# A written order of 3,359 operations, replaced by another; shared buffers handed out in that order

## The chip, the core and the metric

The kernel runs on one core of a Trainium2 chip. A core has a matrix engine (TensorE, PE in the views, its weight loads PEld), VectorE (DVE), ScalarE (ACT), GpSimd (POOL) and SyncE (SP, which here only issues DMAs). Each engine takes its own instructions one after the other; between engines, semaphores hold an instruction back until what it needs is there. The metric is the device time of one execution in microseconds, lower is better.

## The reference

```python
# q, k, v: (4, 8, 768, 64); centroids: (8, 16, 64)
q_assign = argmax(einsum('bhsd,hcd->bhsc', q_n, c_n)); k_assign = the same for k
mask   = q_assign[..., :, None] == k_assign[..., None, :]
scores = where(mask, q @ k.T / 8, -1e9)
attn   = softmax(scores) @ v
x      = attn.transpose(0, 2, 1, 3).reshape(3072, 512)
h      = x @ w_in                       # 512 -> 2048
g      = h * tanh(softplus(h))          # mish
out    = g @ w_out                      # 2048 -> 512
```

So there are two parts: attention in which a query sees the keys of its own cluster alone, and a two-layer network over the 3,072 tokens.

## The kernel before, in words

The attention is cut into 96 units (32 heads, three blocks of 256 queries each); each unit is worked in two halves `a` of 128 queries. A half goes from engine to engine: `scores` (PE, four matmuls into a PSUM tile `s`), `rowmax` (DVE), `expo` (ACT, writes `p`), `total` and `recip` (small), and then:

- in the first 24 units: `p_lo` transposes `p` on PE into PSUM tiles `q`, `ptrans` copies them out on ACT or DVE, `pv` multiplies with the raw values (three parts of PE work for two units);
- in the other 72: `p_hi` (POOL) and `p_lo` (DVE) split `p` into two 16-bit numbers `hl`, `ptrans` transposes those by a DMA from SP's queue (`pt<-hl`), `pv` multiplies them with the split values.

`pv_out` and `x_lo` write the result as `x`. The network follows on the same engines, interleaved with the attention: `m1(j, fi)` is a block of 12 matmuls of the first layer (two blocks `fi` fill one PSUM tile `h`), `e_mish(j)` the activation on ACT, `e_gh` (POOL) and `e_gl` (DVE) split it, `m2(k, a, f)` is a block of six matmuls of the second layer, `m_out` and `m_store` bring a result out. The last part of the network goes by Strassen-like products (`c_*`, `l_*`, `n_*`, `k_*`) with `n_mul` and `k_mul` as their matmul blocks. During the first 24 units the weights are loaded and split (`w_load`, `w_abs`, `w_low`, `w_f32`, `w_sq`, `w_hi`, `w_lo`), and for every four heads the clusters are worked out (`assign_*`). For the first head, `hot_direct` brings the cluster pattern into the operands.

Tiles come from pools with a fixed number of buffers. The PSUM tiles matter here: `s` has two, `h` shares two with `q`, and the tile of the second layer and that of `pv` have one each. A new tile waits until a buffer is given back, that is until the last reader of its former tile has run.

The order is written out by hand. Every operation is entered by `pl.at(t, fn, ...)` with a place `t`, worked out from the tables `T`, `N` and, for single operations, `SHIFT`. `Plan.run` sorts by `t` and traces the operations one after the other; an operation that needs another first (`pl.after`) pulls it forward. `tie` then fixes, for each engine, the order in which its instructions were traced. Nothing else decides what an engine does next. Two facts of the code matter for ScalarE:

```python
        if j % 2 == 0 and j <= 72:
            nc.scalar.preload_act_table_set("mish")
        nc.scalar.activation(st["u", j], st["h", j], AF.Mish, scale=vst[j // 24, "h"])
        if j % 2 and j < 72:
            nc.scalar.preload_act_table_set("natural_log_exp_and_others")
```

so the table for `Mish` is loaded before an even `e_mish` and that for `Exp` after an odd one. In the order before, no `expo` stands between the two; where one does, each of the two functions finds the other's table and a load is put in front of it.

Of the kernel before, what the change touches and what calls it, by code (L numbers as in the profile page):

```python
# [25 lines left out]

class Plan:
# [45 lines left out]
def tile_clustered_attention_mish_ffn(  # L73
# [9 lines left out]
    nc = tc.nc  # L83
    pool = lambda name, bufs, **kw: ctx.enter_context(tc.tile_pool(name=name, bufs=bufs, **kw))
# [22 lines left out]
    pl = Plan(tc)  # L107
# [998 lines left out]
    def k_mul(t, n, f):  # L1106
# [3 lines left out]
        if f == 0:  # L1110
# [3 lines left out]
            else:  # L1114
                banks(("k", t))
                ring("k_12", t)
# [130 lines left out]
    for n in range(32):  # L1247
        p = n // 16
        t = N["w"][n]
# [311 lines left out]
SHIFT = {  # L1561
    ('expo', 11, 0): -0.001, ('w_load', 10): -0.351, ('pv_out', 18): -0.443, ('scores', 24, 1): -0.221,
    ('copy_b', 8): 0.081, ('scores', 25, 1): -1.54, ('w_lo', 2): 0.002, ('p_lo', 26, 1): 3.011,
    ('scores', 6, 0): 0.46301, ('recip', 29, 0): 0.006, ('assign_mm', 0): 5.035, ('qk_load', 0): -4.812,
    ('qk_load', 1): 0.018, ('qk_load', 2): -7.858, ('qk_load', 3): 0.077, ('w_f32', 29): 3.258, ('w_low', 18): 0.746,
    ('w_low', 22): -0.606, ('pv', 5, 0): 0.121, ('w_low', 19): -0.124, ('pv_out', 10): 6.683,
    ('v_split', 1, 1): 0.554, ('recip', 8, 1): 0.081, ('recip', 1, 1): 5.617, ('w_hi', 10): -0.185,
    ('rowmax', 18, 1): 0.004, ('total', 7, 1): 0.2, ('w_low', 29): 0.475, ('w_low', 31): 0.855,
    ('total', 14, 1): 0.656, ('w_load', 0): 0.797, ('p_hi', 7, 0): -1.238, ('p_hi', 6, 1): -0.098,
    ('p_hi', 6, 0): 0.511, ('w_low', 21): 3.895, ('pv', 11, 0): 1.133, ('w_f32', 17): -0.084, ('p_hi', 0, 0): 0.06,  # L1570
    ('p_hi', 0, 1): -0.176, ('p_hi', 1, 0): -1.304, ('p_hi', 1, 1): -0.022, ('p_hi', 2, 0): 0.43,
    ('p_hi', 2, 1): -0.009, ('p_hi', 3, 1): -0.009, ('p_hi', 4, 1): -0.002, ('p_hi', 5, 1): -0.01,
# [738 lines left out]
```

## Time and profile before

| | |
|---|---|
| time before, median of 3 runs | 858.68 us (856.95 to 859.97) |
| profiled execution, first to last instruction | 858.6 us |
| PE / DVE / ACT / POOL busy | 837.1 / 702.6 / 520.9 / 428.0 us |
| granted TensorE clock | 1.00 of full speed (the 2.4 GHz level) |
| first score block begins | 15.61 us |
| last matmul, last VectorE operation, last DMA issue | 852.28 (24 matmuls to 855.06), 855.11, 855.62 us |

The profiled execution is the span itself; nothing is shown around it. A busy PE is not a full one: matmuls overlap, and the span of a matmul of 256 columns (0.27 us) is shown while the next one starts 0.11 us later. So an idle gap in the views is a little shorter than the work that was lost in it.

### The profile page before, as it was taken

The numbers are of one execution on the slowest core, as the hardware profiler recorded it, in microseconds if no ns is written. First come the engines' busy times: TensorE is split into PE (matmuls) and PEld (weight loads), VectorE is DVE, ScalarE is ACT, GpSimd is POOL, SyncE is SP. The second block draws the span as 40 slices with busy tenths as digits, with TensorE's granted clock in tenths as the row PEclk, the third lists the DMA queues.
The fourth block names the chain that finished last, engine by engine and source line by source line (L and its number), as shares of the span: only waits on it lengthen the run. The fifth ranks groups of instructions, "written<-read, shape, count | busy, mean of one in ns | idle before, by whom it ended". The sixth has DMA issues, their size and how long they took to land.

```text
span 858.6 us, 17602 instructions
## 1 busy us (share of the span) xinstructions
PE 837.1 (97%) x6742; PEld 621.0 (72%) x6743; DVE 702.6 (82%) x1225; ACT 520.9 (61%) x885; POOL 428.0 (50%) x410
## 2 busy tenths in 40 slices
PE   8999899999999999999999999999999999999998
PEld 3776676776777777776776776776777776788887
DVE  7989989898889798788877798788978777699851
ACT  6878887765665666564565665465565564356520
POOL 1464665786567546556566447566566444110000
PEclk9999999999999999999999999999999999999999
DMA  9855672398889987897789977988887876000010
GB/s 348 262 173 165 193 209 54 73 180 170 149 153 194 193 154 133 156 184 141 145 177 181 172 157 120 171 155 165 130 159 136 139 137 128 24 1 2 1 44 32
DMA packets 253060, 121.51 MB, mean 142 GB/s; under 512 B 230288, under 2 KB 230800, under 8 KB 252976
## 3 DMA queue, kind: packets, MB, share of 16 engines
q1 hardware_dynamic: 247632, 108.46, 61.1%
q10 hardware_dynamic: 5344, 11.93, 6.3%
q8 instruction: 53, 0.87, 0.4%
q14 instruction: 31, 0.25, 0.1%
HBM read 35.72 MB, written 6.29 MB: 49 GB/s over the span
## 4 chain that ended last, share of the span: by engine, by line
PE 70%; DVE 13%; issue 5%; ACT 4%; DMA 4%; POOL 3%; ACTq 0%; POOLq 0%; DVEq 0%; SPq 0%
PE h L832 8%; PE h L833 8%; PE h L834 8%; PE o L753 8%; PE O L969 6%; PE O L971 6%; PE O L970 6%; PE s L631 5%; PE s L636 5%; DVE m L648 4%; PE cn L922 2%; DVE hl L717 2%; DMA pt<-hl 2%; ACT p L662 2%; PE as L543 1%
## 5 line engine op out<-in xcount | busy, mean ns | idle before, releaser
L662 ACT ACTIVATE p<-s,m 128x768 f32<-128x768 f32 x192 | 172.6, 899 | 161.4 <-DVE m L648 108.0
L700 POOL TENSOR_SCALAR hl<-p,l 128x768 f16<-128x768 f32 x144 | 167.1, 1163 | 168.0 <-DVE l L682 74.2
L648 DVE TENSOR_REDUCE m<-s 128x1 f32<-128x768 f32 x192 | 181.4, 949 | 30.2 <-PE s L636 28.1
L717 DVE SCALAR_TENSOR_TENSOR hl<-p,l,hl 128x768 f16<-128x768 f32 x144 | 172.4, 1202 | 12.2 <-POOL hl L700 11.7
L832 PE MATMUL h<-x,w 128*128 128x256 f16 x640 | 175.6, 274 | 1.5 <-ACT u L843 0.8
L833 PE MATMUL h<-x,w 128*128 128x256 f16 x640 | 174.4, 273 | 0.0
L834 PE MATMUL h<-x,w 128*128 128x256 f16 x640 | 174.4, 273 | 0.0
L631 PE MATMUL s<-A,B 128*128 128x384 f32 x384 | 117.3, 386 | 1.8 <-DMA B<-T 0.8
L969 PE MATMUL O<-w,g 128*128 128x512 f16 x288 | 109.6, 380 | 0.0
L971 PE MATMUL O<-w,g 128*128 128x512 f16 x288 | 109.2, 379 | 0.0
L970 PE MATMUL O<-w,g 128*128 128x512 f16 x288 | 109.2, 379 | 0.0
L636 PE MATMUL s<-Z,T 80*128 80x384 f32 x384 | 99.2, 339 | 0.4 <-issue 0.4
L832 PEld LDWEIGHTS <-w 128*128 128x128 f16 x768 | 75.1, 98 | 26.9 <-issue 17.3
L849 POOL TENSOR_SCALAR g<-u,mscg 128x512 f16<-128x512 f32 x72 | 70.3, 980 | 38.4 <-ACT u L843 36.0
L857 DVE SCALAR_TENSOR_TENSOR g<-u,mscg,g 128x512 f16<-128x512 f32 x72 | 75.5, 1050 | 12.2 <-POOL g L849 11.9
L833 PEld LDWEIGHTS <-w 128*128 128x128 f16 x768 | 75.5, 98 | 11.1 <-issue 1.6
L753 PE MATMUL o<-pt,v 128*64 128x256 f16 x1296 | 79.3, 274 | 3.6 <-DMA pt<-hl 3.0
L834 PEld LDWEIGHTS <-w 128*128 128x128 f16 x768 | 75.2, 98 | 8.6
L753 PEld LDWEIGHTS <-v 128*64 128x64 f16 x1296 | 68.4, 110 | 14.1 <-issue 9.6
L631 PEld LDWEIGHTS s<-A,B 128*128 128x128 f32 x384 | 61.9, 190 | 15.8 <-issue 4.9
L636 PEld LDWEIGHTS s<-Z,T 80*128 80x128 f32 x384 | 69.7, 189 | 0.9 <-DMA Z<-stg 0.7
L843 ACT ACTIVATE u<-h,msch 128x512 f32<-128x512 f32 x80 | 52.1, 685 | 25.0 <-PE h L834 14.5
(242 smaller groups left out, 1366.3 us busy)
## 6 DMA issues: line engine op xcount, KB each, us to landing
qk<-in_qk_dram SPq DMA_DIRECT2D x32, 384.0 KB, 4.6
stage<-in_w_in_dram SPq DMA_DIRECT2D x16, 512.0 KB, 6.6
stage<-in_w_out_dram SPq DMA_DIRECT2D x16, 512.0 KB, 4.5
vraw<-in_vP_dram SPq DMA_DIRECT2D x16, 384.0 KB, 5.2
T<-A ACTq DMA_DIRECT2D x30, 192.0 KB, 3.0
Z<-B SPq DMA_DIRECT2D x30, 192.0 KB, 3.4
B<-T ACTq DMA_DIRECT2D x28, 192.0 KB, 3.4
out_dram<-osb SPq DMA_DIRECT2D x18, 256.0 KB, 2.7
```

Source lines behind the costliest of these rows:

```text
L631: nc.tensor.matmul(s[:, j, :384], st["B", n][:, q0 : q0 + P], st["A", n][:, j * 384 : (j + 1) * 384], start=True, stop=False,)
L636: nc.tensor.matmul(s[:, j, :384], st["T", n][: D + NCL, q0 : q0 + P], st["Z", n][: D + NCL, j * 384 : (j + 1) * 384], start=False, stop=True,)
L648: nc.vector.tensor_reduce(m, st["s", i, a][:, :, :384], axis=AX.XY, op=ALU.max, negate=True)
L662: nc.scalar.activation(p.rearrange("p (n x) -> p n x", n=2), st["s", i, a][:, :, :384], AF.Exp, bias=st["m", i, a], scale=1.0, accum_out=l,)
L700: nc.gpsimd.tensor_scalar(t[:, 0], p, r, 1.0, op0=ALU.mult, op1=ALU.mult)
L717: nc.vector.scalar_tensor_tensor(t[:, 1], p, r, t[:, 0], op0=ALU.mult, op1=ALU.subtract)
L753: nc.tensor.matmul(o[s * D : s * D + D, :256], v if early else v[:, int(part == 1)], st["pt", 2 * m + s][:, :, c + (0 if early or part < 2 ...
L832: nc.tensor.matmul(o, wh, xh, start=(c == 0), stop=False)
L833: nc.tensor.matmul(o, wh, xl, start=False, stop=False)
L834: nc.tensor.matmul(o, wl, xh, start=False, stop=(c == 3))
L969: nc.tensor.matmul(o, gh, wh, start=(f == 0 and fi == 0), stop=False)
L970: nc.tensor.matmul(o, gh, wl, start=False, stop=False)
```

## The change

No instruction is added to the program by hand, and none is taken out or reshaped: all 3,359 operations stand with the same work in another order. `pl.at` no longer uses its `t`: it looks the place up in `RANK`, built from one long string `ORDER`. `SHIFT` goes. As every operation stands behind those that it needs, `pl.after` pulls nothing forward any more.

A new class `Ring` wraps each pool and notes when a tile of a tag is asked for; `tie` makes the first instruction of each such tile follow the first one of the tag's tile before, so that buffers are handed out in the order of `ORDER`. The function `ring`, which held back three of the last stage's operations until a buffer's former user had been traced, goes with its three calls.

```diff
+class Ring:
+    def __init__(self, pool, asked, traced):
+        self.pool, self.asked, self.traced = pool, asked, traced
+
+    def tile(self, *args, tag=None, **kw):
+        if tag is None:
+            return self.pool.tile(*args, **kw)
+        self.asked.append((len(self.traced), (id(self), tag)))
+        return self.pool.tile(*args, tag=tag, **kw)
...
     def at(self, t, fn, *args):
         op = fn.__name__, *args
-        self.ops[op] = (t + SHIFT.get(op, 0), len(self.ops), fn, args)
+        self.ops[op] = (RANK[op], len(self.ops), fn, args)
...
-        for ins in self.traced[self.seen :]:
+        for n, ins in enumerate(self.traced[self.seen :], self.seen):
+            while self.asked and self.asked[0][0] <= n:
+                _, key = self.asked.pop(0)
+                if self.taken.get(key, ins.name) != ins.name:
+                    self.tc.add_manual_dep(ins, self.taken[key], order, reason="tile order")
+                self.taken[key] = ins.name
...
-    rings = []
-
-    def ring(*last):
-
-        while len(rings) >= 3 and pl.state.get(rings[-3]) != "done":
-            pl.after(rings[-3])
-        rings.append(last)
...
-        ring("c_low", f)
...
-        ring("l_sl", f)
...
-                ring("k_12", t)
...
-SHIFT = {
-    ('expo', 11, 0): -0.001, ('w_load', 10): -0.351, ('pv_out', 18): -0.443, ('scores', 24, 1): -0.221,
...
+ORDER = """
+qk_load 0, qk_load 2, qk_load 1, qk_load 3, put_consts, centroids, prep_hi 0, prep_lo 0, copy_z 0, cent_put, copy_t 0,
+prep_hi 1, copy_t 1, w_load 4, w_load 2, v_load 0 0, w_load 0, w_load 5, v_load 0 3, w_load 1, v_load 0 2, w_load 3,
+w_load 6, v_load 0 1, w_load 16, w_load 8, w_load 7, qk_load 7, w_load 10, w_load 9, w_load 12, assign_mm 0, prep_lo
+1, copy_z 1, assign_turn 0, assign_max 0, assign_hot 0, assign_back 0, assign_put 0, copy_a 1, copy_a 0, copy_b 1,
+w_abs 4, copy_b 0, w_abs 2, v_sq 0 0, hot_direct 0, assign_stg 0, hot_direct 1, hot_copy 0, scores 0 0, scores 0 1,
...
+moe_scale_h 0, scores 24 1, pv 11 0, pv 11 1, total 21 0, recip 21 0, pv 11 2, scores 25 1, m1 0 0, m1 0 1, m1 1 0,
+scores 26 0, scores 26 1, m1 1 1, m1 2 0, m1 2 1, m1 3 0, m1 3 1, rowmax 24 1, total 24 0, recip 24 0, p_hi 24 0, w_hi
...
+prep_lo 20, p_hi 56 1, assign_put 5, m2 3 0 4, scores 58 1, pv 27 0, e_mish 32, expo 57 1, expo 57 0, copy_t 20, p_lo
...
+e_mish 33, pv_out 56, pv_out 57, expo 60 0, expo 60 1, p_lo 59 1, x_lo 56, x_lo 57, p_lo 59 0, total 60 1, recip 60 1,
...
+k_mul 1 3 7, k_12 1, k_low 0, m_store 8 1, k_right 0, n_store 0, n_store 1, k_low 1, k_right 1
+"""
+
+RANK = {}
+for _n, _op in enumerate(" ".join(ORDER.split()).split(", ")):
+    _name, *_args = _op.split()
+    RANK[_name, *map(int, _args)] = _n
```

Read engine by engine, the two orders compare so (the old one sorted by its places and with what is pulled forward, the new one as written). PE has 908 blocks in each.

| place | before | after |
|---|---|---|
| PE work in front of `m1 0 0` | ... `scores 24 0` | also `scores 24 1`, `scores 25 0`, `scores 25 1`, `p_lo 23 1`, `pv 11` |
| first 24 units, PE blocks between a half's `scores` and its `p_lo` | 3 to 5 for 33 of 48 | 6 to 10 for 33 of 48 |
| PE blocks between the last `scores` of units 60 and 61 and `pv 30` | 4 `scores`, 5 `m1`, 2 `m2`, 3 parts of `pv` | 4 `scores`, 8 `m1`, 6 `m2`, 3 parts of `pv` |
| the same for `pv 34` | 4 `scores`, 5 `m1`, 2 `m2`, 3 parts of `pv`, 1 `assign_put` | 4 `scores`, 6 `m1`, 6 `m2`, 3 parts of `pv`, 1 `assign_put` |
| first-layer tiles `h` whose first block stands at most two `m1` blocks (or as much PE work) behind the last block of the tile that frees its buffer | 3, all in the last part | 24, of them 9 before `m1 72` |
| pairs `e_mish` even, odd with an `expo` between | 0 | 10 |
| ScalarE between `cent_put` and `hot_direct 0` | `v_sq 0 2`, `prep_hi 1`, `copy_a 0`, `copy_b 0`, `v_sq 0 3`, `v_sq 0 1` | `copy_t 0`, `prep_hi 1`, `copy_t 1`, `copy_a 1`, `copy_a 0`, `copy_b 1`, `w_abs 4`, `copy_b 0`, `w_abs 2`, `v_sq 0 0` |
| neighbours on PE of different kinds (of 907) | 55 more than after | |
| pairs of halves (up to 11 places apart) that one engine takes in the other sequence than the next: `rowmax` and `expo`; `p_lo` and `ptrans` | 5; 0 | 23; 18 |
| `n_mul 7` | before the first `k_mul` | among the last `k_mul` |
| last entries of SP's queue | `m_store 8 1`, `n_store 0`, `n_store 1`, `k_low 0`, `k_right 0`, `k_low 1`, `k_right 1` | `k_low 0`, `m_store 8 1`, `k_right 0`, `n_store 0`, `n_store 1`, `k_low 1`, `k_right 1` |

## Rows read from the trace of the kernel before

**Rows 1.** Page, engines: busy us, share of the span, instructions.

```profile
PE 837.1 (97%) x6742; PEld 621.0 (72%) x6743; DVE 702.6 (82%) x1225; ACT 520.9 (61%) x885; POOL 428.0 (50%) x410
```

**Rows 2.** Windows: length, busy time of PE, PEld, DVE, ACT, POOL, clock, DMA.

```profile
0.00:20.00 20.00, 16.51 (x73) 6.75 (x75) 15.10 (x38) 13.83 (x24) 2.71 (x10) 1.00 0.93 345
...
20.00:140.00 120.00, 113.68 (x904) 83.56 (x905) 110.81 (x201) 97.91 (x193) 64.94 (x81) 1.00 0.62 187
140.00:180.00 40.00, 35.70 (x281) 27.69 (x282) 37.30 (x69) 29.75 (x54) 28.75 (x27) 1.00 0.50 94
...
180.00:740.00 560.00, 556.10 (x4458) 401.88 (x4453) 455.95 (x757) 330.22 (x539) 325.77 (x285) 1.00 0.83 154
...
820.00:859.00 39.00, 35.07 (x322) 31.09 (x319) 9.23 (x18) 3.99 (x7) 1.44 (x2) 1.00 0.12 41
```

**Rows 3.** Waits of PE, 20 to 180 us: total us, times, longest.

```profile
PE q L710 <- ACT p L662: 2.9, 8, 0.9
PE gram L296 <- DVE w L276: 2.4, 3, 1.4
...
PE h L832 <- ACT u L843: 0.8, 1, 0.8
...
PE h L832 <- DVE pt L729: 0.7, 1, 0.7
```

**Rows 4.** Waits of PE, 180 to 740 us.

```profile
PE o L753 <- DMA pt<-hl: 2.6, 3, 1.3
PE s L631 <- DMA B<-T: 0.8, 1, 0.8
```

**Rows 5.** Timeline of PE around the first part of `pv 30`.

```profile
460.81 0.27 PE L834 MATMUL h<-x,w 128*128 128x256 f16 x1
461.01 0.30 PE L753 MATMUL o<-pt,v 128*64 128x256 f16 x1
462.60 0.63 PE L753 MATMUL o<-pt,v 128*64 128x256 f16 x8 [1.29 <-DMA pt<-hl]
```

**Rows 6.** Page, costliest groups: the links from a score block to its value product, and `Mish`.

```profile
L662 ACT ACTIVATE p<-s,m 128x768 f32<-128x768 f32 x192 | 172.6, 899 | 161.4 <-DVE m L648 108.0
L700 POOL TENSOR_SCALAR hl<-p,l 128x768 f16<-128x768 f32 x144 | 167.1, 1163 | 168.0 <-DVE l L682 74.2
L648 DVE TENSOR_REDUCE m<-s 128x1 f32<-128x768 f32 x192 | 181.4, 949 | 30.2 <-PE s L636 28.1
L717 DVE SCALAR_TENSOR_TENSOR hl<-p,l,hl 128x768 f16<-128x768 f32 x144 | 172.4, 1202 | 12.2 <-POOL hl L700 11.7
...
L843 ACT ACTIVATE u<-h,msch 128x512 f32<-128x512 f32 x80 | 52.1, 685 | 25.0 <-PE h L834 14.5
```

**Rows 7.** Chain that ended last: start, us, its three transposing DMAs.

```profile
250.84 5.33 DMA pt<-hl
...
456.86 5.70 DMA pt<-hl
...
522.21 5.45 DMA pt<-hl
```

**Rows 8.** DMA issues of `ptrans`: median us from issue to landing.

```profile
pt<-hl SPq DMA_TRANSPOSE x144, 4.0
```

**Rows 9.** Groups of ScalarE by line: its table loads.

```profile
L842 ACT ACT_TABLE_LOAD x37 | 47.5, 1283 | 0.7
L845 ACT ACT_TABLE_LOAD x36 | 46.2, 1283 | 0.6
```

**Rows 10.** Timeline of ScalarE before the first scores.

```profile
7.65 0.26 ACT L207 COPY C<-ct 64x128 f32<-64x128 f32 x1 [0.36 <-PE ct L201]
8.40 0.84 ACT L368 ACTIVATE vq<-vraw 128x768 bf16<-128x768 f32 x1 [0.48 <-DMA vraw<-in_vP_dram]
...
10.19 0.83 ACT L508 CAST A<-A 64x768 fp32r<-64x768 f32 x1
...
14.70 0.59 ACT L600 ACTIVATE Z<-put 16x512 fp32r<-16x512 f32 x1 [0.91 <-PE put L589]
...
16.89 0.65 ACT L259 ACTIVATE w<-stage 128x512 f32<-128x512 f32 x1
```

**Rows 11.** Timeline of the end: the last DMA issue.

```profile
855.62 0.33 SPq L1178 DMA_DIRECT2D out_dram<-ko  x1
```

More of the change, by code (lines that the diff above doesn't have):

```diff
@@ L34, in __init__ @@
         self.seen = len(self.traced)
+        self.asked = asked
+        self.taken = {}
         self.last = {}
@@ new lines @@
+rowmax 0 0, rowmax 0 1, v_sq 0 3, w_abs 0, hot_copy 1, expo 0 0, expo 0 1, p_hi 0 1, w_low 0, p_hi 0 0, p_lo 0 0,
+scores 1 0, total 0 1, w_low 5, w_low 4, w_low 1, w_low 2, w_f32 0, v_sq 0 2, w_abs 1, ptrans 0 0, rowmax 1 0, scores
+1 1, p_lo 0 1, rowmax 1 1, expo 1 0, ptrans 0 1, expo 1 1, w_f32 1, w_f32 2, p_hi 1 1, p_hi 1 0, w_sq 0, scores 2 0,
+p_lo 1 0, w_sq 1, scores 2 1, p_lo 1 1, rowmax 2 0, v_sq 0 1, v_max 0, ptrans 1 0, rowmax 2 1, expo 2 0, w_f32 4,
+ptrans 1 1, expo 2 1, total 1 1, w_low 3, w_low 16, prep_hi 2, w_low 8, w_low 6, total 2 1, prep_lo 2, copy_z 2,
@@ new lines @@
+expo 4 0, ptrans 3 1, w_f32 10, expo 4 1, p_hi 4 1, p_hi 4 0, w_sq 5, scores 5 0, p_lo 4 0, scores 5 1, pv 1 0, w_f32
+7, w_f32 8, w_abs 12, w_abs 9, copy_a 2, rowmax 5 0, recip 3 1, rowmax 5 1, expo 5 0, copy_t 3, ptrans 4 0, w_f32 9,
+expo 5 1, total 1 0, pv 1 1, pv 1 2, total 0 0, recip 0 0, recip 1 0, p_hi 5 0, p_lo 4 1, w_sq 6, scores 6 0, p_lo 5
+0, p_hi 5 1, w_low 13, total 4 1, w_low 12, total 5 1, prep_lo 3, w_f32 12, pv_out 2, w_abs 13, recip 5 1, ptrans 4 1,
+w_abs 11, pv_out 3, w_low 11, rowmax 6 0, ptrans 5 0, x_lo 3, scores 6 1, w_sq 7, p_lo 5 1, expo 6 0, rowmax 6 1,
@@ new lines @@
+ptrans 5 1, w_f32 11, w_f32 13, recip 4 1, expo 6 1, x_lo 2, p_hi 6 1, p_hi 6 0, scores 7 1, w_sq 8, p_lo 6 0, scores
+7 0, p_lo 6 1, pv 2 0, pv 2 1, pv 2 2, w_load 15, qk_load 5, w_load 14, qk_load 4, copy_z 3, qk_load 6, hot_copy 3,
+w_load 19, w_load 21, v_load 1 0, v_load 1 3, w_load 22, w_load 18, total 3 0, w_abs 15, ptrans 6 0, rowmax 7 1, w_abs
+14, w_abs 17, total 6 1, w_low 15, w_low 17, w_low 14, rowmax 7 0, ptrans 6 1, w_f32 17, w_abs 16, w_f32 16, w_f32 15,
+copy_b 3, expo 7 0, w_f32 14, expo 7 1, pv_out 4, p_hi 7 1, recip 3 0, total 4 0, recip 4 0, total 2 0, recip 2 0,
@@ new lines @@
+9 1, copy_t 4, pv_out 6, w_abs 22, pv_out 7, x_lo 6, x_lo 7, p_hi 9 0, p_hi 9 1, total 9 1, w_low 22, total 8 1,
+assign_put 1, p_lo 9 0, scores 10 0, p_lo 9 1, w_sq 16, scores 10 1, total 6 0, recip 6 0, ptrans 9 0, assign_stg 1,
+recip 8 1, recip 9 1, rowmax 10 0, w_hi 0, ptrans 9 1, rowmax 10 1, expo 10 0, expo 10 1, w_abs 18, w_lo 0, w_f32 21,
+w_f32 19, w_f32 18, p_hi 10 1, p_hi 10 0, pv 4 0, pv 4 1, scores 11 0, pv 4 2, scores 11 1, p_lo 10 0, p_lo 10 1,
+copy_z 4, copy_a 4, hot_copy 4, w_load 23, w_load 20, w_load 25, total 9 0, recip 9 0, copy_b 4, w_hi 1, w_lo 1,
@@ new lines @@
+rowmax 11 0, pv_out 8, w_hi 2, ptrans 10 0, expo 11 0, x_lo 8, prep_hi 5, total 10 1, prep_lo 5, pv_out 9, rowmax 11
+1, expo 11 1, w_low 23, total 11 1, w_low 25, w_low 20, w_lo 2, ptrans 10 1, w_abs 20, copy_t 5, x_lo 9, total 7 0,
+recip 7 0, p_hi 11 0, p_hi 11 1, scores 12 0, w_sq 17, p_lo 11 0, w_sq 18, w_sq 19, scores 12 1, p_lo 11 1, scores 13
+0, rowmax 12 0, w_hi 3, w_f32 22, recip 11 1, expo 12 0, ptrans 11 0, w_lo 3, rowmax 12 1, w_abs 25, ptrans 11 1,
+recip 10 1, w_hi 4, expo 12 1, w_abs 23, total 8 0, recip 8 0, p_hi 12 1, p_hi 12 0, pv 5 0, pv 5 1, scores 13 1, p_lo
@@ new lines @@
+12 0, pv 5 2, p_lo 12 1, scores 14 0, scores 14 1, qk_load 8, copy_z 5, w_load 24, qk_load 11, hot_copy 5, v_load 1 2,
+w_load 26, w_load 29, w_load 31, w_load 27, w_load 28, w_load 30, w_lo 4, w_f32 20, copy_b 5, w_hi 5, rowmax 13 0,
+rowmax 13 1, ptrans 12 0, expo 13 0, expo 13 1, copy_a 5, w_low 24, total 12 1, prep_hi 6, w_lo 5, recip 12 1, w_f32
+23, pv_out 10, ptrans 12 1, pv_out 11, total 13 1, w_low 26, w_low 29, x_lo 11, p_hi 13 0, w_sq 20, w_sq 21, w_sq 22,
+p_lo 13 0, w_sq 23, rowmax 14 0, ptrans 13 0, w_abs 24, expo 14 0, rowmax 14 1, w_f32 24, p_hi 13 1, x_lo 5, p_lo 13
@@ new lines @@
+1, total 10 0, recip 10 0, ptrans 13 1, p_hi 14 0, scores 15 0, pv 6 0, pv 6 1, p_lo 14 0, rowmax 15 0, w_abs 26, w_hi
+6, expo 15 0, expo 14 1, w_f32 25, w_f32 26, w_lo 6, ptrans 14 0, recip 13 1, copy_t 6, w_abs 29, w_hi 7, v_sq 1 0,
+p_hi 14 1, scores 15 1, scores 16 0, total 11 0, recip 11 0, p_hi 15 0, p_lo 14 1, pv 6 2, w_sq 24, w_sq 25, p_lo 15
+0, w_sq 26, scores 16 1, rowmax 15 1, rowmax 16 0, ptrans 14 1, w_f32 29, expo 15 1, w_lo 7, ptrans 15 0, pv_out 12,
+pv_out 13, p_hi 15 1, total 12 0, recip 12 0, x_lo 10, total 14 1, prep_lo 6, w_low 31, w_low 28, w_low 27, w_low 30,
```

962 lines of the change are left out of this document (276 added, 686 removed), and 37 rows, old and new, of the table SHIFT.

## The prediction, made before the change was run

> **What bounds the kernel now.** Read the page's engine line first: PE is busy for 837.1 of 858.6 us [rows 1]. The change neither adds nor drops a matmul, so all that it can move is the 21.5 us in which PE stands, and what hides inside the overlapped spans. The windows then say where that time lies [rows 2]: 3.5 us before 20 us, 6.3 us from 20 to 140, 4.3 us from 140 to 180, 3.9 us in the 560 us from 180 to 740, nothing from there to 820, and about 3.5 us at the end. The clock column is 1.00 in every stretch.
>
> The first 180 us are another kernel than the rest. There DVE is busy for 110.8 of 120 and 37.3 of 40 us [rows 2]; PE has no first-layer work to fall back on before `m1 0 0`, so the two wait for each other in turns. From 180 us on DVE has 104 us to spare in 560, and PE stops for single late things. The waits name them: early, transposes that wait for `expo` (2.9 us in 8 waits) and the gram blocks for DVE's `w_f32` (2.4 in 3) [rows 3]; later, three value products that wait for a transposing DMA (2.6) and one score block for a copy (0.8) [rows 4]. The timeline shows that idle time understates a stop: at `pv 30` the wait is put at 1.29 us, but the second matmul starts 1.59 us after the first, where neighbours stand some 0.1 to 0.2 apart [rows 5].
>
> **The change part by part.** The same blocks run on PE, so its work is taken as unchanged. What a block costs more behind another kind is seen at 460.81: the value product starts 0.20 us after the last first-layer matmul [rows 5], against 0.11 inside a block. The new order has 55 changes of kind fewer; at 0.09 each that would be 5 us, but most of them lie between first layer and scores, which no row here prices. I take nothing for it, with a gain of 2 us as the bound I believe.
>
> *Late transfers, 180 to 740 us.* From a score block to its value product the links are `rowmax` 0.95, `expo` 0.90, `p_hi` 1.16, `p_lo` 1.20 [rows 6] and the DMA, 4.0 us as a median [rows 8]: 8.2 us with nothing queued. But on the chain the transposes took 5.3 to 5.7 us [rows 7], and two halves share each engine, another 1.2: 11 us. What stands between the last scores and the product, in PE time: a block `m1` is 12 matmuls of 0.11, so 1.3 us; `m2` six of twice the columns, 1.3; a part of `pv` 0.7; a score block 0.7 by the same spacing. For `pv 30` that is 14.0 us before and 23.1 after; for `pv 34` 14.4 and 20.9. Over the 36 late products, the nine shortest distances were 13.0 to 14.7 us; after, one is 13.4 and the next 16.1. So two of the three waits of [rows 4] should go (the third stood at 19.5 us and stands at 19.7). With what the idle column leaves out: -2.5 us, between 0 and -4.4 (all four waits, 3.4, and some 0.25 each).
>
> *140 to 180 us.* `m1 0 0` stood in front of work that was ready sooner, and PE stopped 0.7 us there and 0.8 before `m1 2 0` [rows 3]. Now `scores 24 1`, `25 0`, `25 1`, a transpose block and the whole of `pv 11` stand before it: some 6.3 us of PE work that runs while the last `x` and the first `Mish` are made. I take -2.5 of the 4.3 us that PE stands in this stretch; bounds 0 and -4.3.
>
> *20 to 140 us.* Between a half's scores and its transposes stand mostly 6 to 10 blocks in place of 3 to 5, which is the cover for the 2.9 us of [rows 3]. Yet DVE must do the same work here and is 92% busy, so what PE no longer waits for `expo` it may wait for something else: -2.0, bounds 0 and -5.
>
> *The start.* ScalarE now has ten operations between `cent_put` and `hot_direct 0`: six casts (0.83 each), a scaling copy about as long, two `w_abs` (0.65) and a squaring (0.84) [rows 10], 7.9 us from 7.91. `hot_direct` then starts at 15.8 in place of 14.70, and the first complete scores with it. Three of the casts belong to head 1 and were done later before, so part of it comes back: +1.0, bounds 0 and +1.5.
>
> *Table loads.* Ten pairs of `e_mish` now have an `expo` between them: 20 more loads of 1.283 us [rows 9], 25.7 us on an engine that is 61% busy [rows 1]. In the stretch where they lie ScalarE has 230 us free [rows 2], and the product and the second layer behind them stand 8 us and more away. I take nothing; without that cover it is 1.3 us each time that PE waits for the table, at most 25.7.
>
> The Trainium skill (ScalarE: Activation LUTs, "Table sets: the hidden batching unit") says to do all of one set's work before switching, and puts a switch at about 2.66 us with the drain, not at 1.28 ("What ACT_TABLE_LOAD costs"). By its figure the 20 loads would take an estimated 53 us of ScalarE, which still fits into its free time; the idle time in front of the loads here, 0.7 and 0.6 us in all [rows 9], shows no drain of that size before them.
>
> *Short reuses of `h`.* 24 first-layer tiles, in place of 3, begin within two blocks (2.6 us) of the last matmul on the buffer that they take. Each needs `Mish` to read it first, 0.69 us [rows 6]. That fits if ScalarE is free; if it is just in an `expo`, PE stands up to 0.9 us. ScalarE spends 172.6 of 858.6 us in `expo` [rows 6], a fifth, and half of one is left on average: 24 times 0.2 times 0.45 is 2.2, of which the 0.6 us that a block of 1.3 leaves over covers about half. I take +1.0, bounds 0 and +11 (below).
>
> *The end.* The last DMA issue, at 855.62 [rows 11], is followed by 3.0 us to the end. It stays last, but behind five other stores that are written close before it: +0.5, bounds 0 and +2.
>
> Sum: -2.5 - 2.5 - 2.0 + 1.0 + 1.0 + 0.5 = -4.5, from 858.6: **854.1 us**. The profiled execution is 0.1 us under the median of the runs, so nothing is corrected.
>
> **The rivals.** *More comes of it.* If DVE's 9.2 idle us from 20 to 140 close as well and all late waits go, it is -4.4 - 4.3 - 5 + 1 + 0.5, about -12: 846. For it: all distances grew. Against it: DVE cannot be hurried, and the start is later.
>
> *Nothing comes of it.* The first 180 us are set by DVE's 148 us of work, which is the same; a wait removed in front of one PE block turns up before the next. Then the late transfers alone (-2.5) stand against start, end and `h`: 858.6. For it: PE's waits early are many and small [rows 3].
>
> *Slower: the queues disagree.* In the old order halves pass `rowmax`, `expo`, `p_hi`, `p_lo`, `ptrans` nearly in one sequence: 5 pairs change places between the first two, none between the last two. In the new one it is 23 and 18. An engine that reaches a half whose input comes second waits for it, and all behind it wait too. ScalarE then comes late to a `Mish`, and of 24 short reuses of `h` each costs an `expo` of 0.90 or more. It decides from where ScalarE is over 0.6 us late (a block of 1.3 less 0.69) at about half of them: 12 times 0.9, +11, less the gains that still come: 865. Against it: ScalarE has 230 us free from 180 on. The Trainium skill (PSUM — Partial Sum Buffer, "Engine vs sequencer instructions") states that the queues of ScalarE, VectorE and GpSimd are strict first in, first out; no row here tells against it.
>
> That the change does nothing is no rival: every engine's order is another.
>
> **How the numbers follow.** A measurement of this kernel tells about 0.3% from no change, 2.6 us. Chances: the forecast (851 to 856) 0.45, more (841 to 851) 0.13, nothing (856 to 861) 0.17, slower (861 and above, about 865) 0.25. So faster 0.58, same 0.17, slower 0.25. The range is 841 to 867: down to the larger gain with the 2 us of cheaper changes of kind and the 3 us of stops hidden inside overlapped spans (a dozen early waits at 0.25), up to the slower case with the end's bound; it leaves out less than two in ten. The forecast's own range is 850 to 858.
>
> **What would show it.** Right: PE's idle time from 140 to 180 us halves; among the waits after 180 us `pv` on the transposing DMA is down to one; 93 or 94 table loads with PE not waiting for `expo` or `Mish`; the first scores begin about 1 us later. Wrong: PE waits of `h` on `u`, ten or more; SP or GpSimd waiting on a half out of turn, with `pv` late again; idle time of DVE from 20 to 140 us no smaller. The clock column at 1.00 throughout is assumed: the stretches of PE's standing get shorter, not longer.

## The result, and the profile after

The new order takes 865.07 us (median of 5 runs, 863.58 to 867.64) beside 858.59 for the old one (856.95 to 859.97): a ratio of 1.0073, 95% interval 1.0052 to 1.0095, so 6.5 us slower. The profiled execution has a span of 863.7 us and is the run of 865.47: a time is 1.7 to 1.8 us longer than its span, in all runs. The old kernel's span of 858.6 was therefore an execution of some 860.3, as slow as the slowest of the others; that the forecast's base still met the median is chance.

The page's engine line (busy us, share, instructions) answers to [rows 1]:

```profile
PE 837.4 (97%) x6742; PEld 626.0 (72%) x6743; DVE 677.5 (78%) x1225; ACT 545.6 (63%) x905; POOL 414.3 (48%) x410
```

PE is busy for the same 837 us, so nearly all of the 5.1 us between the two spans is standing time: 26.3 us in place of 21.5. ScalarE has 20 instructions more, the table loads. The windows (length, busy time of PE, PEld, DVE, ACT, POOL, clock, DMA) answer to [rows 2]:

```profile
0.00:20.00 20.00, 15.63 (x70) 6.43 (x72) 14.13 (x37) 12.74 (x20) 1.39 (x8) 1.00 0.93 345
20.00:140.00 120.00, 112.64 (x915) 86.50 (x914) 113.99 (x205) 102.02 (x205) 70.03 (x86) 1.00 0.64 187
140.00:180.00 40.00, 38.39 (x299) 30.16 (x297) 36.52 (x67) 28.46 (x48) 27.31 (x26) 1.00 0.54 103
180.00:740.00 560.00, 550.90 (x4399) 398.99 (x4400) 429.66 (x758) 354.21 (x555) 308.08 (x284) 1.00 0.82 154
...
820.00:864.00 44.00, 40.01 (x367) 35.61 (x364) 13.71 (x27) 4.48 (x10) 1.45 (x2) 0.98 0.12 43
```

PE stands 4.4 us before 20 us (3.5 before), 7.4 from 20 to 140 (6.3), 1.6 from 140 to 180 (4.3) and 9.1 from 180 to 740 (3.9). The loss lies in the long stretch in which the old order hardly stopped. PE's waits from 180 to 740 us (total us, times, longest) answer to [rows 4]:

```profile
PE o L777 <- DMA pt<-hl: 4.7, 5, 1.8
PE s L655 <- ACT p L686: 3.2, 5, 1.0
PE h L856 <- ACT u L867: 0.6, 1, 0.6
```

The second kind was there before too, but hardly (kernel before, the same stretch):

```profile
PE s L631 <- ACT p L662: 0.2, 1, 0.2
```

Value products wait more for transposing DMAs, not less; score blocks wait 3.0 us more for `expo` to give back an `s`; the short reuses of `h` cost 0.6 us once. The longest stop is at `pv 22`. Its halves are 44 0 to 45 1. Timeline of VectorE (the `p_lo` of 45 0, then of 44 1), of SP (the transposes of 44 1, 45 0 and 45 1) with the landing of the three, then of PE, then the windows around it:

```profile
312.13 1.44 DVE L741 SCALAR_TENSOR_TENSOR hl<-p,l,hl 128x768 f16<-128x768 f32 x1 [0.36 <-POOL hl L724]
...
314.48 1.00 DVE L741 SCALAR_TENSOR_TENSOR hl<-p,l,hl 128x768 f16<-128x768 f32 x1
```

```profile
315.78 8.32 SPq L757 DMA_TRANSPOSE pt<-hl  x3
...
DMA to landing us min/median/max: 5.2/6.0/6.5
```

```profile
324.03 0.30 PE L777 MATMUL o<-pt,v 128*64 128x256 f16 x1
326.12 3.79 PE L777 MATMUL o<-pt,v 128*64 128x256 f16 x35 [1.79 <-DMA pt<-hl]
```

```profile
322.00:324.00 2.00, 2.00 (x17) 1.65 (x16) 0.96 (x1) 1.94 (x4) 0.76 (x2) 1.00 1.13 138
324.00:326.00 2.00, 0.33 (x2) 0.21 (x2) 1.86 (x3) 1.97 (x3) 1.04 (x2) 1.00 0.94 196
326.00:330.00 4.00, 3.88 (x37) 3.64 (x37) 0.67 (x1) 0.86 (x2) 3.91 (x4) 0.57 0.53 98
330.00:334.00 4.00, 4.00 (x36) 3.52 (x35) 2.98 (x9) 3.03 (x5) 0.80 (x1) 1.00 0.25 52
```

VectorE finishes 45 0 first, but SP's queue has 44 1 first, so the finished half stands 4.7 us, until 318.30. The three transposes go out within 4.3 us of each other and take 5.2 to 6.5 us to land, where 4.4 is the median of all 144, and PE waits for the last, 45 1. Behind the stop the granted clock is 0.57 over 4 us, so that 35 matmuls take 3.79 us where 2.15 is usual: a stop of 2 us costs near 3.7. The clock is not the loss of the kernel, though: three of the five runs had a mean granted clock of 1.000 and took 864.63 to 867.64 us.

ScalarE's table loads by line (busy, mean ns, idle time in front and what ended it) answer to [rows 9]:

```profile
L866 ACT ACT_TABLE_LOAD x37 | 47.5, 1283 | 2.4 <-DMA T<-A 1.8
L869 ACT ACT_TABLE_LOAD x36 | 46.2, 1283 | 0.6
L686 ACT ACT_TABLE_LOAD x10 | 12.8, 1283 | 10.1 <-DVE m L672 7.4 <-DVE l L698 2.5 <-DMA pt<-hl 0.2
L867 ACT ACT_TABLE_LOAD x10 | 12.8, 1283 | 3.1 <-DVE g L881 1.4 <-PE h L858 1.4 <-DVE l L698 0.2
```

The 20 that are new (the last two lines) run behind the wait of the `expo` or `Mish` that needs them: the row maximum is there, and only then the load begins.

ScalarE's own waits from 180 to 740 us, first of the kernel before, then after:

```profile
ACT p L662 <- DVE m L648: 99.4, 53, 4.3
...
ACT u L843 <- PE h L834: 11.2, 9, 1.9
...
ACT x L790 <- PE o L753: 4.1, 5, 1.3
```

```profile
ACT p L686 <- DVE m L672: 43.6, 28, 3.8
ACT u L867 <- PE h L858: 33.4, 26, 4.1
ACT x L814 <- PE o L777: 26.5, 16, 4.4
```

Before, ScalarE stood at an `expo`, whose input comes from VectorE; a `Mish` or `pv_out` behind it mostly found its matmuls done. Now it stands 60 us at those two, waiting for PE itself. That this alone makes an `expo` behind them late is not shown: in the tenth run below ScalarE stands longer there (74.3 and 42.2 us), and no score block waits for `expo`.

### The profile page after: what moved, and what is told of

It is laid out like the page before. It is cut to its first block, busy times and chain, and to the rows that moved or that the text cites. A ratio compares the mean times of both kernels' runs of the same rounds, so it can differ in the third digit from the quotient of the medians.

```text
span 863.7 us, 17574 instructions
## 1 busy us (share of the span) xinstructions
PE 837.4 (97%) x6742; PEld 626.0 (72%) x6743; DVE 677.5 (78%) x1225; ACT 545.6 (63%) x905; POOL 414.3 (48%) x410
## 4 chain that ended last, share of the span: by engine, by line
PE 75%; DVE 12%; DMA 6%; ACT 3%; issue 2%; POOL 1%; ACTq 0%; SPq 0%; DVEq 0%; POOLq 0%
PE o L777 11%; PE h L856 8%; PE h L858 8%; PE h L857 8%; PE s L655 6%; PE O L993 6%; PE O L995 6%; PE O L994 6%; PE s L660 6%; DMA pt<-hl 5%; DVE m L672 3%; PE q L734 2%; DVE hl L741 2%; PE cn L946 2%; ACT p L686 1%
## 5 line engine op out<-in xcount | busy, mean ns | idle before, releaser
L724 POOL TENSOR_SCALAR hl<-p,l 128x768 f16<-128x768 f32 x144 | 163.0, 1135 | 177.0 <-DVE l L706 57.0
L672 DVE TENSOR_REDUCE m<-s 128x1 f32<-128x768 f32 x192 | 179.5, 949 | 26.1 <-PE s L660 24.6
L741 DVE SCALAR_TENSOR_TENSOR hl<-p,l,hl 128x768 f16<-128x768 f32 x144 | 169.5, 1187 | 32.2 <-POOL hl L724 32.1
L777 PE MATMUL o<-pt,v 128*64 128x256 f16 x1296 | 81.1, 278 | 5.2 <-DMA pt<-hl 4.7
L873 POOL TENSOR_SCALAR g<-u,mscg 128x512 f16<-128x512 f32 x72 | 57.8, 808 | 51.5 <-ACT u L867 44.3
L777 PEld LDWEIGHTS <-v 128*64 128x64 f16 x1296 | 70.2, 111 | 16.1 <-issue 10.2
L881 DVE SCALAR_TENSOR_TENSOR g<-u,mscg,g 128x512 f16<-128x512 f32 x72 | 58.5, 819 | 10.9 <-POOL g L873 10.8
```

The costliest lines, as they stand in the source:

```text
L672: nc.vector.tensor_reduce(m, st["s", i, a][:, :, :384], axis=AX.XY, op=ALU.max, negate=True)
L724: nc.gpsimd.tensor_scalar(t[:, 0], p, r, 1.0, op0=ALU.mult, op1=ALU.mult)
L741: nc.vector.scalar_tensor_tensor(t[:, 1], p, r, t[:, 0], op0=ALU.mult, op1=ALU.subtract)
L777: nc.tensor.matmul(o[s * D : s * D + D, :256], v if early else v[:, int(part == 1)], st["pt", 2 * m + s][:, :, c + (0 if early or part < 2 ...
```

## The experiments

All ratios are to the old kernel, run on the same chip. For an order made of two, the edit is written as what `ORDER` becomes.

### Where the loss is made

**1.** `e1_one_sequence`:

```diff
-x_lo 41, x_lo 40, p_lo 43 0, total 44 0, rowmax 44 1, recip 44 0, p_lo 42 1, rowmax 45 0, p_lo 43 1, ...
-ptrans 42 0, v_load 2 1, m_store 1 0, ptrans 43 0, v_load 3 1, ptrans 42 1, ptrans 43 1, ... expo 45 0, expo 44 1,
+x_lo 41, x_lo 40, p_lo 42 1, total 44 0, rowmax 44 1, recip 44 0, p_lo 43 0, rowmax 45 0, p_lo 43 1, ...
+ptrans 42 0, v_load 2 1, m_store 1 0, ptrans 42 1, v_load 3 1, ptrans 43 0, ptrans 43 1, ... expo 44 1, expo 45 0,
```

> The new order with one thing undone: from unit 24 on, rowmax, expo, total, recip, p_hi, p_lo and ptrans keep their places, but the halves go through all of them in the sequence in which PE writes their scores (370 of 3,359 places hold another half). PE's order and the places of the table loads are the same. If halves out of turn make the transposes late, the stop of 2.5 us at pv 22 and those at scores 60, pv 42 and scores 89 go, and the time falls by 3 to 5 us, to 860 to 862. If the 20 table loads or the places of the blocks on PE cost the time, it stays at 864 to 866.

861.19 us, 1.0052 (1.0032 to 1.0073). In its profile `pv` waits 1.6 us for the DMA from 180 to 740 us, where the new order waits 4.7, and `pv 22` no longer stops for 2 us. The three transposes, in sequence there, land within 4.2 to 5.4 us. By the medians about a third of the loss is gone; the waits of scores on `expo` are 2.7 us, from 3.2:

```profile
PE s L655 <- ACT p L686: 2.7, 5, 1.0
PE o L777 <- DMA pt<-hl: 1.6, 3, 1.0
```

**2 to 4.** Two orders joined:

```diff
-ORDER = new
+ORDER = new[:1118] + rest of old    # e2
+ORDER = old[:1118] + rest of new    # e3
+ORDER = new[:862] + rest of old     # e4
```

> The first 1,118 operations of the new order (to 236 us of its profile, m2 0 1 5), then the others in the old sequence. By the two traces, compared at equal work of PE, the new order is neither ahead nor behind at 236 us: 858 to 859. If the early part leaves a debt that the traces hide: 862 or more.

857.74 us, 1.0008 (0.9989 to 1.0028).

> The first 1,118 operations of the old order (to scores 35 1, 235 us), then the others in the new sequence. If the loss is made behind 236 us, at single stops, the time is that of the new order, 863 to 865. If it is made in the first 236 us: 858 to 859. With the run before this one the two changes should add up to the whole of +6.5 us.

865.37 us, 1.0089 (1.0066 to 1.0111).

> The first 862 operations of the new order (to m1 3 1, 170 us), then the others in the old sequence. At equal work of PE the new order is 4.3 us ahead at 176 us. If that lead is time won, it holds with the old sequence behind it: 854 to 856. If it is only work of PE done sooner whose inputs come no sooner, it is paid back within 25 us as in the new order: 858 to 859.

858.33 us, 1.0005 (0.9991 to 1.0019).

All of the loss is made behind 236 us. The second and fourth also carry `Ring` with the old sequence behind their cut and lose nothing by it. The lead of 4.3 us at 176 us is no gain: in the fourth run's profile the next product stops for it.

```profile
175.07 0.30 PE L777 MATMUL o<-pt,v 128*64 128x256 f16 x1
177.78 3.28 PE L777 MATMUL o<-pt,v 128*64 128x256 f16 x35 [2.42 <-DMA pt<-hl]
```

### Does distance help?

**5.** `e5_first_come`: PE's order as in the first, the late units' softmax instructions each at the place where its input was ready by that run's trace (the rule by which the order was sorted):

```diff
+key[op] = ready(op) if op is rowmax, expo, total, recip, p_hi, p_lo or ptrans and 236 < start(op) < 728 else start(op)
```

> As the first experiment (new order of PE, halves in one sequence), and from 236 to 728 us each rowmax, expo, total, recip, p_hi, p_lo and ptrans also stands in its engine's queue where its input was ready by that experiment's trace, ahead of what began later. PE's order is again that of the new kernel. If waiting in the queue behind an instruction whose input is late is what the new order loses, the stops of scores on p and of pv on the transposing DMA behind 236 us shrink further and the time is 857 to 859. If PE's new order, the table loads or the distances cost it, it stays at 861 or above.

901.59 us, 1.0493 (1.0464 to 1.0523): scores wait 15.0 us for `expo`. Sorting by a trace of other waits sets up new ones; it also split more `Mish` pairs (919 instructions of ScalarE, 14 more loads than in the new order). Nothing follows from it on the queues by themselves.

**7, 8, 14, 15.** Products later on PE by two blocks of `m1` or `m2`: 32 of the 36 (e7, e15 in the old order, e8 in that of the fourth run) or `pv 12` alone (e14, in that of the fourth run), `pv_out` and `x_lo` moved as much in the written order (e7, e8) or by the trace's times (e14, e15). PE's order at `pv 12` in e14:

```diff
-scores 27 0, m2 0 0 0, scores 27 1, pv 12 0, pv 12 1, pv 12 2, scores 28 0, m1 4 0, m1 4 1, m2 0 0 1, m1 5 0,
+scores 27 0, m2 0 0 0, scores 27 1, scores 28 0, m1 4 0, m1 4 1, pv 12 0, pv 12 1, pv 12 2, m2 0 0 1, m1 5 0,
```

> The old order with one thing changed: 32 of the 36 late value products stand two blocks of m1 or m2 (2.6 us) later on PE, with their pv_out and x_lo as much later in their queues. This is the forecast's gain by distance alone. If distance was worth what the forecast took for it, 855 to 856. If a transposing DMA is late in any execution only by chance, or what follows (x_lo, the pt buffers) loses as much, 857 to 858.

907.5 us, 1.0563 (1.0533 to 1.0594).

> The fourth experiment's order (new to 170 us, then old) with the 32 late value products two blocks later. There pv 12 stopped PE for 2.6 us and TensorE's clock stood at half for some 4 us behind it. If that stop took the lead of 4.3 us that the new order has at 176 us, it is gone here and the time is 853 to 856. If the lead is only work done ahead of its inputs, the stop turns up at another place: 857 to 859.

903.39 us, 1.051 (1.0474 to 1.0545).

> The fourth experiment's order with pv 12 alone moved two blocks (3.9 us) later on PE, and its pv_out and x_lo behind the instructions that then come sooner. In 8 of 12 runs of that experiment the mean clock was under 1.00, and in its profile pv 12 stopped PE for 2.6 us with half the clock for 4 us behind it. If that stop is where the lead of 4.3 us goes, 854 to 856, faster than both kernels. If not, 857 to 859.

864.13 us, 1.0058 (1.0037 to 1.008).

> The old order with 32 of its 36 late value products two blocks of m1 or m2 later on PE (3.5 us in the middle, with the scores between), and their pv_out and x_lo moved on ScalarE and VectorE behind all that began before the new end of the product. Distance alone. If the forecast's step was right, 855 to 856. If distance doesn't help because what waits is set by the queues in front, 857 to 859. If a later product holds up ScalarE as in the seventh experiment, above 862.

899.7 us, 1.0474 (1.0452 to 1.0497).

Every one is slower. The fourteenth shows it at one product. `pv 12` no longer stops, and the next one, `pv 13`, does (PE's timeline):

```profile
188.75 0.62 PE L655 MATMUL s<-A,B 128*128 128x384 f32 x2 [0.62 <-ACT p L686]
189.20 0.52 PE L660 MATMUL s<-Z,T 80*128 80x384 f32 x2
193.54 2.77 PE L777 MATMUL o<-pt,v 128*64 128x256 f16 x24 [3.81 <-DVE x L838]
```

There is one tile `o`: `pv 13` needs the result of `pv 12` read by `pv_out` and `x_lo`. Behind this stop of 3.81 us the granted clock is 0.50 from 193 to 197 us, which is part of what the run lost. The last `x_lo` (L838) now stands on VectorE behind work of other halves, one piece of which waits for GpSimd:

```profile
192.01 1.02 DVE L741 SCALAR_TENSOR_TENSOR hl<-p,l,hl 128x768 f16<-128x768 f32 x1 [0.47 <-POOL hl L724]
193.06 0.43 DVE L838 SCALAR_TENSOR_TENSOR x<-o,x 64x256 f16<-64x256 f32 x1
```

In the fifteenth, ScalarE stands at `pv_out` for 68.7 us where it stood 4.1 in the old kernel (its waits from 180 to 740 us):

```profile
ACT x L814 <- PE o L777: 68.7, 22, 6.6
ACT p L686 <- DVE m L672: 67.6, 39, 4.2
```

The distance itself did arrive: from the timelines, the margin between the last landing and a product's start is 5.8 us in the middle, in place of 0.8. But PE's waits show that the scores pay for it:

```profile
PE s L655 <- ACT p L686: 9.7, 10, 1.5
PE s L655 <- DVE stg L634: 6.0, 2, 3.3
PE s L655 <- DMA B<-T: 4.2, 2, 2.7
```

In the three runs with 32 products moved PE is also busy for 849.8 to 850.9 us, 13 more than before, at a mean granted clock of 0.990 to 0.992: part of the loss is matmuls at the lower clock behind such stops.

### Table loads

**6 and 16.** More loads, 22 in the new order (116 in place of 94) and 20 in the old (94 in place of 74):

```diff
+        if j in (7, 9, 11, 13, 15, 33, 43, 45, 57, 59):
+            nc.scalar.preload_act_table_set("mish")                          # e16: the two lines swapped
+            nc.scalar.preload_act_table_set("natural_log_exp_and_others")
         nc.scalar.activation(st["u", j], st["h", j], AF.Mish, scale=vst[j // 24, "h"])
```

> The new kernel with 20 more table loads: two in front of each of ten odd Mish (7, 9, 11, 13, 15, 33, 43, 45, 57, 59), at or near the places where the new order already has 20 more than the old. If those loads are part of the loss, as many again cost as much again: 867 or more. If ScalarE's free time takes them: 864 to 866, the time of the new kernel.

879.0 us, 1.0225 (1.0197 to 1.0254): by the ratios 13 us over the new order.

> The old kernel with 20 more table loads: Exp's and Mish's in front of the same ten odd Mish (7, 9, 11, 13, 15, 33, 43, 45, 57, 59). Without its 73 loads the old order was 2.2 us faster, 0.03 us for each. If loads are as cheap as that in an order that goes in one sequence, 858 to 860. If 20 loads cost what they cost the new order in the sixth experiment (14 us), 870 or more; if they cost the 3 us that the loads are part of the new order's loss, 861 to 863.

879.1 us, 1.0233 (1.0203 to 1.0263): 20.7 us over the old one, from 25.7 us of loads. PE's waits from 180 to 740 us in it, against 0.2 us of the first kind before:

```profile
PE s L631 <- ACT p L662: 11.1, 7, 3.0
PE O L974 <- DVE g L860: 3.8, 3, 2.5
```

So ScalarE, busy for 63% of its time here, hides little of 2.6 us put in front of a `Mish` that is due: the `expo` behind it is late, and so is the next score block.

**9 and 10.** No table loads (but one at the start), in the old order and in the new; the activation is left out:

```diff
-        if j % 2 == 0 and j <= 72:
-            nc.scalar.preload_act_table_set("mish")
-        nc.scalar.activation(st["u", j], st["h", j], AF.Mish, scale=vst[j // 24, "h"])
-        if j % 2 and j < 72:
-            nc.scalar.preload_act_table_set("natural_log_exp_and_others")
+        nc.scalar.activation(st["u", j], st["h", j], AF.Copy, scale=vst[j // 24, "h"])
...
-        nc.scalar.activation(dst, src, AF.Mish, scale=vst[B - 1, "h"])
+        nc.scalar.activation(dst, src, AF.Copy, scale=vst[B - 1, "h"])
```

> The old kernel with every Mish replaced by a plain scaling copy, and without its table loads (one load is left at the start): the network's activation is left out, the instructions keep their shapes. It is the base for the next run. If the old order hides its 73 loads, 857 to 859; if they cost it time as well, less.

856.65 us, 0.9973 (0.996 to 0.9986).

> The new kernel with the same replacement: no table loads in either. If the 20 loads that the new order adds are its whole loss, it takes what the run before takes, within 1 us. If the queues out of turn are the loss and the loads nothing, it takes 5 to 7 us more than the run before. If both count, 2 to 4 us more.

859.94 us, 1.0018 (1.0 to 1.0037): 3.3 us over the run before (3.9 by the ratios), where the two whole kernels are 6.5 apart (6.3). So some 2.4 to 3.2 us go with the loads, but the four intervals together leave 2.7 us either way: the times alone don't tell this share from nothing. PE's waits are plainer: without loads no score block waits for `expo` from 180 to 740 us, where the new kernel's waited 3.2 us with the same order. What remains is `pv` on the DMA, 2.1 us in the ninth and 5.8 in the tenth:

```profile
PE o L777 <- DMA pt<-hl: 5.8, 7, 1.3
PE s L655 <- DVE stg L634: 0.4, 1, 0.4
```

**11 and 12.** The loads written out, in the new order and in that of the first experiment:

```diff
-        if j % 2 == 0 and j <= 72:
+        if TABLE[j][0]:     # the ScalarE operation before that needs a table is an expo
             nc.scalar.preload_act_table_set("mish")
...
-        if j % 2 and j < 72:
+        if TABLE[j][1]:     # the next one is an expo
```

> The new kernel with the same order and about as many loads (92), but the ten splits' loads are written out: Exp's directly behind the even Mish, Mish's directly in front of the odd one. In the new kernel the 20 that the compiler puts in stand behind the wait of the expo or Mish that needs them (idle time of 10.1 and 3.1 us in front of them) and add 1.28 us to each chain. If that place is what they cost, 860 to 863. If only their number counts, or nothing of them, 864 to 866.

864.92 us, 1.0075 (1.0044 to 1.0106).

> The first experiment (halves in one sequence) together with the loads written out as in the run before. If the two are separate parts of the loss, their gains add up: 857 to 859, the time of the old kernel, with PE's new order. If both remove the same stops, 860 to 862.

863.4 us, 1.005 (1.0032 to 1.0068). Where the load stands, before or behind the wait, makes no difference that shows.

**13.** The edits of 1 and 10 together.

> The new order with halves in one sequence (first experiment) and with Mish replaced by a scaling copy, without table loads (the activation is left out). The old kernel took 856.65 us so changed, the new one 859.94. If sequence and loads are two parts that add up, 2 us come off: 857 to 858, the old order's time within a us. If the two are the same stops, it stays at 859 to 860, and some 3 us of the loss have another cause, PE's own new order.

861.42 us, 1.0037 (1.0018 to 1.0056): not under the tenth. The two gains don't add up. Without loads the halves' sequence shows no gain; 3.3 us (10) to 4.8 us (13) over the ninth remain that neither explains.

### What a half waits for

From the timelines, for the 136 halves of units 28 to 95: the time from the end of a half's scores to its landed transpose, as means of the time that it stands in front of each link and of the DMA itself (us). Rows 1 and 17 are the runs of these numbers.

| | rowmax | expo | total | recip | p_hi | p_lo | issue | DMA | whole, with the links' own work |
|---|---|---|---|---|---|---|---|---|---|
| before | 1.13 | 1.08 | 1.16 | 0.06 | 1.22 | 1.57 | 0.42 | 4.35 | 15.59 |
| after | 0.91 | 1.85 | 1.63 | 0.91 | 1.60 | 1.65 | 0.95 | 4.58 | 18.62 |
| 1 | 0.93 | 1.73 | 1.60 | 0.96 | 1.45 | 1.69 | 0.76 | 4.60 | 18.28 |
| 17 | 1.06 | 1.75 | 1.68 | 0.03 | 2.09 | 1.98 | 0.98 | 4.53 | 18.69 |

**17 and 18.** `recip` behind its `total`, in the new order and in that of the first experiment:

```diff
-total 44 1, total 45 0, e_gl 16, recip 45 0, p_lo 44 0, recip 44 1, e_gl 17, rowmax 45 1,
+total 44 1, recip 44 1, total 45 0, recip 45 0, e_gl 16, p_lo 44 0, e_gl 17, rowmax 45 1,
```

> The new order with one thing changed: from unit 24 on each recip stands directly behind the total of its half on VectorE (86 of 144 stood apart; in the old order 1). Two instructions of 0.2 us that follow each other can't hold up much else. If the 0.85 us that a half waits there on average makes the transposes late, the pv waits on the transposing DMA shrink and the time falls by 2 to 4 us, to 861 to 863. If those waits are taken up by other waits of the same half further on, 864 to 866.

864.95 us, 1.0085 (1.0065 to 1.0106).

> The first experiment's order (halves in one sequence, 861.2 us) with each recip directly behind its total. If the gap in front of recip is the rest of the loss, 858 to 859, the old order's time. If it is not, 861 to 862.

861.9 us, 1.0051 (1.0033 to 1.0068). The table's last row says why: the 0.88 us gained in front of `recip` are stood off in front of `p_hi` and `p_lo`. Beside each other, the two runs show once more what the sequence of halves is worth: 3.0 us.

No whole version beat the old kernel; the best, the second and the fourth, equal it.

## Why the prediction was wrong

The sign was missed: 854.1 was forecast, 865.07 came. By stretches of PE's standing time:

- *Start*, +1.0: measured +0.9, and the first scores 1.2 us later. The number is right, but by luck: it was worked out from ScalarE's queue, and VectorE made it. The new order has VectorE do head 1's `prep_lo 1` and `copy_z 1` before head 0's `assign_turn 0`, so head 0's pattern `hott` comes 1.2 us later and PE's `put` waits for it; ScalarE's `hot_direct` came only 0.3 us behind its input. VectorE's `hott` before, then after, with PE's wait:

```profile
12.92 0.98 DVE L574 STREAM_TRANSPOSE hott<-hot 128x768 bf16<-128x768 bf16 x1
```

```profile
14.11 0.98 DVE L598 STREAM_TRANSPOSE hott<-hot 128x768 bf16<-128x768 bf16 x1
15.15 0.28 PE L605 MATMUL put<-hott,put_w 128*32 128x256 bf16 x1 [0.72 <-DVE hott L598]
```

- *20 to 140 us*, -2.0: measured +1.1. Wrong in sign and small. The waits of transposes on `expo` did fall (20 to 180 us), from 2.9 us to 0.6 in one, and came back as waits on the copies, 2.3 and 2.1 us, from 0.7 and 1.0, as the rival "nothing" had it: VectorE is busy for 114 of 120 us.
- *140 to 180 us*, -2.5: measured -2.7, the sign named for it. But the work that PE did sooner waits for its inputs behind: counted at equal work of PE (each block at one fixed duration) the lead is 4.3 us at 176 us and 1.1 at 200, and the fourth run, which keeps the stretch, gains nothing. So the sign came, and the gain did not: the next stretch paid it back.
- *Late transfers, 180 to 740 us*, -2.5: this is the step that failed, with the one on table loads. Standing time there rose by 5.2 us, and the waits on the transposing DMA from 2.6 us to 4.7. The step took 11 us from scores to a landed transpose, for old and new, 1.2 of them for standing behind another half. Measured, a half took 15.6 us in the old order, of which it stood 6.6 in front of its links, and 18.6 in the new, of which it stood 9.5. So distances grew and the way grew too: the margin between the last landing and the product's start rose in the middle only from 0.8 to 1.8 us, and the worst went from -1.5 to -2.1 (the product had begun and stopped). The worst is `pv 22`: the forecast's own count has one product left at a short distance, 13.4 us, and by the timelines this is the one, at 13.3; its last transpose landed 15.3 us behind its last scores. Nor was distance free: 7 and 15 cost over 40 us, since one `o`, two `s` and a fixed queue on ScalarE tie a product to what follows.
- *Table loads*, 0 with 25.7 as the bound: wrong. The cover named was ScalarE's 230 free us. But PE waits 3.2 us for `expo` from 180 to 740 us, 0.2 before, and not at all in run 10 without loads. In time, 22 and 20 more loads cost 13 and 21 us in runs 6 and 16, all in front of a `Mish` that was due; for the 20 that the change adds, 9 and 10 leave some 2.4 to 3.2 us, with an interval that reaches nothing. Free time over a stretch hid only 5 of run 16's 25.7 us. The rule cited, that all work of one set is done before switching (the Trainium skill, ScalarE: Activation LUTs, "Table sets: the hidden batching unit"), would have told against the change, and runs 6 and 16 agree with it. The drain that makes a switch 2.66 us on the same page ("What ACT_TABLE_LOAD costs") is not seen: all 94 loads took 1.283 us, with 2.4 and 0.6 us of idle time in all in front of the 73 that are written out.
- *Short reuses of `h`*, +1.0: one wait of 0.6 us, in place of two of 0.7 and 0.8 before. Nothing lost.
- *The end*, +0.5: +0.2, within its bounds; the last DMA issue is followed by 3.1 us, in place of 3.0.
- *PE's work unchanged*: right, 837.4 us busy.

The rival "slower: the queues disagree" named the time, 865, but by another road, so that it met the number is luck. With the loads in, the halves out of turn cost some 2 to 3 us: 1, 12 and 18 have ratios 0.0021, 0.0025 and 0.0034 under the new order, 11 and 17; each interval alone is wide, the three agree. The fourth pair, 10 and 13 without loads, shows no such gain. The road is late transposes at `pv 22` (1 beside the new order); in 17 and 18 products wait 1.9 and 2.1 us for transposes, and there the road is not shown. It is not `h`, at 0.6 us. The rival's condition, a ScalarE that comes late to `Mish`, was mostly the reverse of what happened: ScalarE came early and stood there.

Of the signs, idle time from 140 to 180 us, the loads (94) and the first scores (16.80 in place of 15.61 us) came as named; `pv` waits for DMAs were five, not one, and PE waited seven times for `expo`, 4.2 us. The sign named for a wrong forecast is there too: GpSimd's `p_hi` stands 44.0 us, in place of 24.0, for an `hl` that a transposing DMA has to give back.

What stays open: some 3 to 5 us that are left without table loads (10, 13) and aren't got back by the sequence (13) or, with the loads in, by `recip` (17). In the waits they are late transposes; that PE's new order itself, with scores spread singly, sets up the longer queues is argued from the table, not shown: no run here has PE's old order with the other engines' new one.

## What to carry to other kernels

In a kernel whose bound engine is busy for 97%, the order in the queues of the others is part of its timing: cost a new order by how long a piece of work stands in front of each engine, from the trace, and not by the sum of its links. Free time of an engine is cover only where it lies in front of the instruction in question. Before a distance is lengthened, look for the buffer (here one `o`) whose next user then comes too soon.

## What was not expected of the hardware

- Behind a stop of PE of some 2 us the granted clock fell to 0.50 (the 1.2 GHz level) and came back after about 4 us: at `pv 22` of the new kernel (1.79 us of idle time), `pv 12` of the fourth run (2.42) and `pv 38` of the second (2.25). It isn't certain: in the third, PE stood 2.38 us and the clock stayed at 1.00, as it did behind 3.49 us in the thirteenth and 3.03 us in the sixteenth.

```profile
241.82 0.62 PE L655 MATMUL s<-A,B 128*128 128x384 f32 x2 [2.38 <-ACT p L686]
```

```profile
239.00:242.00 3.00, 0.62 (x4) 0.18 (x2) 0.56 (x2) 2.50 (x4) 2.83 (x3) 1.00 0.92 227
242.00:246.00 4.00, 3.75 (x44) 3.01 (x44) 2.96 (x7) 2.09 (x5) 2.58 (x4) 1.00 0.68 136
```

- The same VectorE instruction took less time in the new order: the 72 that make the second half of `g` took 1050 ns before and 819 after, and GpSimd's 72 in front of them 980 and 808. That is 17 of the 25 us by which VectorE's busy time fell, and the kernel gained nothing by it. Means by line, before and after:

```profile
L857 DVE SCALAR_TENSOR_TENSOR g<-u,mscg,g 128x512 f16<-128x512 f32 x72 | 75.5, 1050 | 12.2 <-POOL g L849 11.9
```

```profile
L881 DVE SCALAR_TENSOR_TENSOR g<-u,mscg,g 128x512 f16<-128x512 f32 x72 | 58.5, 819 | 10.9 <-POOL g L873 10.8
```

- A transposing DMA takes 3.6 to 6.6 us to land in the new kernel's profile, but single ones take far longer. In the second run three in a row took 9.3, 7.1 and 6.6 us (issued at 575.1, 578.4 and 581.8 us), and `pv 38` stopped for the last. No run here shows why. The four of 572 to 583 us:

```profile
DMA to landing us min/median/max: 4.1/6.9/9.3
```
